# Paired rows of F on one partition in the second expert layer's weights

## The chip, the cores and the metric

The kernel runs on one core of one Trainium2 chip. The metric is device microseconds of one execution; lower is better. The kernel before takes 1385.26 us, the median of six runs between 1384.77 and 1387.1 us.

A core has a matrix engine (TensorE, PE in the profile), which multiplies a stationary operand, put in by a LDWEIGHTS instruction (its own row, PEld), with a moving operand that streams past; a vector engine (DVE); a scalar engine (ACT); GpSimd (POOL); and SyncE (SP), which here issues most of the DMAs.

## The reference

A two-dimensional Fourier mixing of 8 sequences of 2496 tokens of 256 features is followed by a mixture of experts, in which each of the 19968 tokens goes to the one of 8 experts whose logit is largest. All numbers are float32.

```python
# x: (8, 2496, 256); w_gate: (256, 8); w1: (8, 256, 1024); w2: (8, 1024, 256)
X = np.fft.fft(np.fft.fft(x, axis=1), axis=2).real.astype(np.float32).reshape(19968, 256)
logits = X @ w_gate
expert_idx = np.argmax(logits, axis=1)
probs = softmax(logits)
...
for e in range(E):                       # tokens of one expert
    h = np.maximum(x_sorted[lo:hi] @ w1[e], 0.0)
    y_sorted[lo:hi] = h @ w2[e]
return gate_w[:, None] * y               # in the order of the tokens
```

The middle dimension, F = 1024, is summed over in the second product. Any order of its 1024 rows gives the same result up to rounding, as long as the columns of `w1[e]` and the rows of `w2[e]` follow the same order.

## The kernel before, in words

The work has two parts that are woven into each other. The first part, batch by batch, computes the Fourier mixing as matmuls (`first`, `second`), finds each token's expert (`route`), and scatters the token's row, with its number and its gate weight, into a table `Xs` in HBM where each expert has its own region. The second part, `experts` (L533), takes blocks of rows of one expert from `Xs` and runs the two layers on them. There are 66 blocks: 28 of 512 rows, 13 of 256 and 25 of 128. The first six are small (two of 256, four of 128), then come four of 256, then 28 of 512, and the last stage has 7 of 256 and 21 of 128, in turn one of 256 and three of 128.

For each block, `fetch` (L507) reads the block's row number and expert from a small table into registers of SP and issues three DMAs on SP's queue: the token rows `xb` from `Xs` (L512), all of the expert's `w1` into `w1_sb` (L515, 1 MB) and all of its `w2` into `w2_sb` (L517, 1 MB). `xb`, `w1_sb` and `w2_sb` have three buffers each, so that up to two blocks ahead are loaded while one is worked on. In the profile both weight tiles are called `w_sb`.

In SBUF a tile lies over 128 partitions. `w1_sb` is [128, 2, 1024]: partition p has rows p and 128 + p of `w1` (the 256 features), each 1024 floats that lie together in HBM. `w2_sb` is [128, 8, 256]: partition p has rows p, 128 + p, ..., 896 + p of `w2`, each a separate run of 256 floats, 1 KB.

A block is computed like this:

- `turn` (L520) turns the rows with matmuls against an identity (tile `pt`, L528) and copies them as `xT` (L529), so that features lie on partitions.
- First layer: for each chunk of 128 of the 1024 columns, two products (`c` = 0, 1, the two halves of the 256 features) sum in PSUM to `ph`, with 128 columns of `w1_sb` as the stationary operand and `xT` as the moving one, as wide as the block has rows (L566). A ReLU writes the result to `hT`, on ACT for even groups (L572) and on DVE for odd ones (L570). `hT[:, f]` holds the chunk f of F on its partitions.
- Second layer: for each 128 rows of the block, eight products sum over the eight chunks to `py`, with `hT[:, f, ...]` as the stationary operand and `w2_sb[:, f]`, 256 wide, as the moving one (L584). ACT scales by the gate weight (L585) and POOL scatters the rows to `out` (L212).

All matmuls that go through the helper `mm` carry its line, L197. A float32 product is issued as two LDWEIGHTS and two MATMULs, so a block has 32 pairs for `ph` and 16 for each `py`.

The order of the instructions on each engine is the order in which the Python program issues them (a manual schedule). `experts` and the Fourier part are generators; the loop at L674 to L688 takes steps of `experts` and, by a count of work due, steps of the Fourier part of the next batch between them. Nothing of this order depends on durations or on the layout of the weights. After the seventh batch's blocks there is no Fourier work left, and the last blocks of 512 and the whole last stage are expert work alone.

Of the kernel before, what the change touches and what calls it, by code (L numbers as in the profile page):

```python
# [49 lines left out]
def bc(ap, axis, n):  # L50
    shape = list(ap.shape)
    shape.insert(axis, n)
    return ap[tuple([slice(None)] * axis + [None])].to_broadcast(shape)
# [138 lines left out]
def kernel(ctx: ExitStack, tc, x, w_gate, w1, w2, out):  # L192
    nc = tc.nc
    vec, act, pool = nc.vector, nc.scalar, nc.gpsimd

    def mm(o, lhsT, rhs, start=True, stop=True, **kw):
        nc.tensor.matmul(o, lhsT=lhsT, rhs=rhs, start=start, stop=stop, **kw)  # L197
# [13 lines left out]
    def put_row(dst, idx, rows, last, group):  # L211
        return unordered(pool.indirect_dma_start(  # L212
            out=dst, out_offset=bass.IndirectOffsetOnAxis(ap=idx, axis=0),
            in_=rows, in_offset=None, bounds_check=last, oob_is_err=False), group)
# [6 lines left out]
    def taken(ins, b):  # L221
        ins = getattr(ins, "ins", ins)
        if b + 1 < B:
            tc.declare_no_dep(ins, group=f"xs{b + 1}", reason="a block has rows of its round's batches alone")
        tc.add_to_no_dep_group("taken", ins)
# [281 lines left out]
    def fetch(b, size, tab, i):  # L507
        n = size // 128
        row = nc.sync.value_load(tab[:, 0, i:i + 1], min_val=0, max_val=ROWS - size)
        ev = nc.sync.value_load(tab[:, 1, i:i + 1], min_val=0, max_val=E - 1)  # L510
        xb = bp.tile([128, BIG // 128, W], F32, tag="xb", name="xb", bufs=3)
        taken(nc.sync.dma_start(out=xb[:, 0:n].rearrange("p t c -> p (t c)"),  # L512
                                in_=Xs[ds(row, size)].rearrange("(p t) c -> p (t c)", t=n)), b)
        w1_sb = bp.tile([128, 2, F], F32, tag="w1", name="w1_sb", bufs=3)
        nc.sync.dma_start(out=w1_sb[:], in_=w1[ds(ev, 1)].rearrange("o (c p) f -> p (o c) f", p=128))  # L515
        w2_sb = bp.tile([128, FC, D], F32, tag="w2", name="w2_sb", bufs=3)
        nc.sync.dma_start(out=w2_sb[:], in_=w2[ds(ev, 1)].rearrange("o (c p) d -> p (o c) d", p=128))  # L517
        return xb, w1_sb, w2_sb

    def turn(size, xb):  # L520

        xT = bp.tile([128, 2, BIG], F32, tag="xT", name="xT", bufs=1)
        n = min(size // 128, 2)
        for h in range(-(-size // 256)):
            pt = pst.tile([128, 2, n, 128], F32, tag="t", name="pt")
            for c in range(2):
                for t in range(n):
                    nc.tensor.transpose(pt[:, c, t], xb[:, 2 * h + t, c * 128:(c + 1) * 128], ident[:])  # L528
            vec.tensor_scalar(xT[:, :, 256 * h:256 * h + 128 * n], pt[:].rearrange("p c t k -> p c (t k)"),  # L529
                              con["alt"][:], None, op0=ALU.mult)  # L530
            yield xT

    def experts(todo):  # L533

        got, xT = [], None

        def fetch_some(k, most=3):

            while k + len(got) < len(todo) and len(got) < most and todo[k + len(got)][:3] in tabs:
                b, size, last, at = todo[k + len(got)]
                got.append(fetch(b, size, tabs[b, size, last], at))

        for k, (b, size, last, at) in enumerate(todo):
            n, m = size // 128, BIG // size
            if not k:
                while todo[0][:3] not in tabs:
                    yield 0
                fetch_some(0)  # L550
                for _ in range(9):
                    yield 0
                for xT in turn(size, got[0][0]):
                    pass
            fetch_some(k)
            xb, w1_sb, w2_sb = got.pop(0)
            turned = iter(())
            follow = todo[k + 1] if k + 1 < len(todo) else None
            ro = bp.tile([128, BIG // 128], I32, tag="ro", name="ro", bufs=4)
            vec.tensor_copy(ro[:, 0:n], xb[:, 0:n, D])  # L560
            hT = bp.tile([128, FC, BIG], F32, tag="hT", name="hT", bufs=1)
            for f in range(FC // m):
                ph = psh.tile([128, m, size], F32, tag="h", name="ph")
                for j in range(m):
                    for c in range(2):
                        mm(ph[:, j], w1_sb[:, c, (m * f + j) * 128:(m * f + j + 1) * 128], xT[:, c, 0:size],  # L566
                           c == 0, c == 1)
                o = hT[:, m * f:m * (f + 1), 0:size]
                if f % 2:
                    vec.tensor_scalar(o, ph[:], 0.0, None, op0=ALU.max)  # L570
                else:
                    act.activation(o, ph[:], ACTF.Relu)  # L572
                yield 1
            if follow:
                while follow[:3] not in tabs:
                    yield 0
                fetch_some(k + 1, 2)
                turned = turn(follow[1], got[0][0])
            y = bp.tile([128, BIG // 128, D], F32, tag="y", name="y", bufs=3)
            for i in range(n):  # L580
                xT = next(turned, xT)
                py = psy.tile([128, D], F32, tag="y", name="py")
                for f in range(FC):
                    mm(py[:], hT[:, f, i * 128:(i + 1) * 128], w2_sb[:, f], f == 0, f == FC - 1)  # L584
                act.activation(y[:, i], py[:], ACTF.Copy, scale=xb[:, i, D + 1:D + 2])  # L585
                put_row(out, ro[:, i:i + 1], y[:, i], NT - 1, "out")
                yield 2
            for xT in turned:
                pass
# [45 lines left out]
    for _ in range(WARM):  # L635
# [9 lines left out]
        out=Xs[E * CAP:].rearrange("(k p) w -> p k w", k=BLK // 128), in_=bc(pad[:], 1, BLK // 128)), "xs"), 0)  # L645
# [24 lines left out]
    for k, _ in enumerate(second(0)):  # L670
        if k % 2 == 0:
            next(early, None)
    work = experts(todo)
    for b in range(1, B):  # L674

# [40 lines left out]
```

## Time and profile before

One execution was taken with the hardware profiler.

| | |
|---|---|
| median of six runs | 1385.26 us |
| the profiled execution's own time | 1381.19 us |
| its span, first to last instruction | 1379.4 us |
| mean granted TensorE clock in it | 0.984 of full |
| HBM read, written | 194.28 MB, 54.83 MB |
| DMA packets | 134517, of them 114438 on the queue that SP issues to (q1) |
| loads of expert weights (w1 and w2) | 132 of 1024 KB |

How to read the profile: a line of the instruction groups has the line of the kernel, the engine, the operation, the tile written and the tiles read, the shapes, the count, then busy time and the mean length of one, and the idle time of the engine before these instructions with what ended it. A wait line has the total in us, how many times, and the longest. The ends of matmuls are modelled, so that one matmul's length overlaps the next one's; the time from start to start is what a matmul really takes of the engine. A weight load can run under the matmul before it. "From issue to landing" is the time from a DMA's issue to its last byte's arrival.

By stretches of the span, DMA's mean busy share is 1.04 from 100 to 150 us, 0.41 from 700 to 750 us, and 0.77 from 1130 to 1370 us.

### The profile page before, as it was taken

To read this page: it belongs to the slowest core of one execution; us is meant where nothing else is said; L and a number is where in the kernel's file an instruction comes from. 1 tells how busy PE (TensorE), PEld (TensorE's weight loads), DVE (VectorE), ACT (ScalarE), POOL (GpSimd) and SP (SyncE) were. 2 spreads that over 40 slices of the span, in tenths; PEclk is the share of its full clock that TensorE was granted. 3 is DMA by queue.
4 is the path that set the end of the run, shared out by engine and by line. 5 is a ranking of instruction groups with operands and counts; after the bars stand their busy time and mean duration, and the time that the engine had idled before them with its cause. 6 is when DMAs were issued, how large, how long until landed. Compare 5 with 4: busy or idle time off the path is not lost.

```text
span 1379.4 us, 17245 instructions
## 1 busy us (share of the span) xinstructions
PE 1320.1 (96%) x6186; PEld 1005.3 (73%) x6186; DVE 382.4 (28%) x1206; ACT 284.0 (21%) x656; POOL 352.1 (26%) x360
## 2 busy tenths in 40 slices
PE   4659999999999999999999999999999999999998
PEld 2548988776777667766777777666776689999997
DVE  3544244432333224122232212224111111111111
ACT  1413132331222113221122112221111111111111
POOL 2254334144132411431112411431311111111111
PEclk9769999999999999999999999999999999999999
DMA  8859967754366343545235142425323428888882
GB/s 233 213 195 325 371 209 223 235 167 183 125 192 186 127 164 122 177 141 174 96 129 167 60 174 92 157 95 179 123 99 105 143 85 274 279 281 280 274 269 92
DMA packets 134517, 248.81 MB, mean 180 GB/s; under 512 B 11245, under 2 KB 93839, under 8 KB 134432
## 3 DMA queue, kind: packets, MB, share of 16 engines
q1 hardware_dynamic: 114438, 194.38, 43.8%
q0 software_dynamic: 19344, 52.37, 11.0%
q10 hardware_dynamic: 650, 0.97, 0.3%
q8 instruction: 49, 0.80, 0.2%
q14 instruction: 36, 0.29, 0.1%
HBM read 194.28 MB, written 54.83 MB: 181 GB/s over the span
## 4 chain that ended last, share of the span: by engine, by line
PE 53%; issue 31%; POOL 7%; DMA 2%; DVE 1%; POOLq 0%; ACT 0%; SPq 0%; ACTq 0%; DVEq 0%
PE py L197 23%; PE ph L197 22%; POOL out_dram L212 5%; PE p L197 4%; PE s L197 2%; POOL Xs L212 2%; PE pt L528 2%; DMA Xs<-rows,pi 1%; DMA w_sb<-in_moe_w_dram 1%; DMA xb<-Xs 0%; POOLq L212 0%; PE rk L197 0%; DVE hT L570 0%; POOLq L711 0%; DVE rows L406 0%
## 5 line engine op out<-in xcount | busy, mean ns | idle before, releaser
L197 PE MATMUL ph<-xT,w_sb 128*128 128x512 f32 (+2 forms) x2112 | 585.3, 431 | 2.2 <-DMA w_sb<-in_moe_w_dram 2.2
L197 PE MATMUL py<-w_sb,hT 128*128 128x256 f32 x2608 | 580.8, 379 | 0.0
L197 PEld LDWEIGHTS py<-w_sb,hT 128*128 128x128 f32 x2608 | 487.3, 190 | 62.0
L197 PEld LDWEIGHTS ph<-xT,w_sb 128*128 128x128 f32 x2112 | 339.9, 191 | 196.6 <-issue 178.2
L212 POOL DMA_INDIRECT out_dram<-y,ro x163 | 159.2, 977 | 828.9 <-ACT y L585 808.8
L570 DVE TENSOR_SCALAR hT<-ph 128x512 f32<-128x512 f32 x163 | 112.7, 691 | 690.3 <-PE ph L197 346.6
L585 ACT ACTIVATE y<-py,xb 128x256 f32<-128x256 f32 x163 | 77.3, 474 | 603.2 <-PE py L197 598.4
L212 POOL DMA_INDIRECT Xs<-rows,pi x160 | 159.7, 998 | 119.2 <-issue 70.9
L572 ACT ACTIVATE hT<-ph 128x512 f32<-128x512 f32 x163 | 97.3, 597 | 331.7 <-PE ph L197 331.7
L529 DVE TENSOR_SCALAR xT<-pt,table 128x512 f32<-128x512 f32 (+1 forms) x94 | 63.3, 673 | 74.2 <-PE pt L528 74.2
L197 PE MATMUL s<-xh,w 104*112 104x256 f32 (+2 forms) x208 | 58.6, 405 | 18.6 <-DVE xh L284 18.5
L197 PEld LDWEIGHTS p<-table,t 120*128 120x128 f32 x352 | 53.8, 201 | 18.4 <-issue 12.0
L404 DVE COPY lg<-p 128x16 f32<-128x16 f32 x80 | 13.9, 174 | 187.2 <-ACT zs L401 187.0
L528 PE MATMUL pt<-table,xb 128*128 128x128 f32 x326 | 51.9, 275 | 11.9 <-DMA xb<-Xs 11.9
L528 PEld LDWEIGHTS pt<-table,xb 128*128 128x128 f32 x326 | 40.4, 142 | 28.5 <-DMA xb<-Xs 13.5
L197 PEld LDWEIGHTS s<-xh,w 104*112 104x112 f32 x208 | 38.1, 197 | 30.5 <-DVE xh L284 14.4
L197 PE MATMUL p<-table,zz 128*128 128x145 f32 (+1 forms) x320 | 55.8, 299 | 3.0 <-DVE rows L406 2.3
L197 PE MATMUL p<-table,t 120*128 120x120 f32 (+1 forms) x352 | 56.2, 285 | 1.8 <-DVE rows L406 1.5
L197 PEld LDWEIGHTS p<-table,zz 128*128 128x128 f32 x320 | 45.5, 194 | 6.5 <-DVE rows L406 2.4
L406 DVE SCALAR_TENSOR_TENSOR rows<-p,zs 128x129 f32<-128x129 f32 x160 | 48.3, 343 | 1.4 <-issue 0.2
L274 POOL DMA_INDIRECT xh<-in_x_dram,ix x24 | 25.0, 1041 | 72.2 <-PE s L197 51.4
L307 ACT COPY t<-s 112x512 f32<-112x512 f32 x48 | 28.0, 584 | 53.8 <-PE s L197 53.8
(84 smaller groups left out, 335.1 us busy)
## 6 DMA issues: line engine op xcount, KB each, us to landing
w_sb<-in_moe_w_dram SPq DMA_DIRECT2D x132, 1024.0 KB, 8.1
xb<-Xs SPq DMA_DIRECT2D x28, 516.0 KB, 3.7
Td<-t SPq DMA_DIRECT2D x24, 448.0 KB, 3.4
xl<-in_x_dram SPq DMA_DIRECT2D x21, 448.0 KB, 9.6
t<-Td SPq DMA_DIRECT2D x8, 720.0 KB, 7.9
t<-Td SPq DMA_DIRECT2D x8, 600.0 KB, 8.7
xb<-Xs SPq DMA_DIRECT2D x13, 258.0 KB, 4.1
xb<-Xs SPq DMA_DIRECT2D x25, 129.0 KB, 2.6
```

What stands on the lines that cost most here:

```text
L197: nc.tensor.matmul(o, lhsT=lhsT, rhs=rhs, start=start, stop=stop, **kw)
L212: return unordered(pool.indirect_dma_start(out=dst, out_offset=bass.IndirectOffsetOnAxis(ap=idx, axis=0), in_=rows, in_offset=None, bounds ...
L274: pool.indirect_dma_start(out=xh[:].rearrange("p j d -> p (j d)"), out_offset=None, in_=xrows, in_offset=bass.IndirectOffsetOnAxis(ap=ix[: ...
L307: act.copy(t1[:, 2 * half:2 * half + 2], ps[:])
L404: vec.tensor_copy(lg[:, k:k + 2], p3[:, NY:NY + 2 * E].rearrange("p (m e) -> p m e", m=2))
L406: vec.scalar_tensor_tensor(rows[:, k + m, 0:NY], p3[:, 0:NY], zs[:, 0:1], zs[:, 1:], op0=ALU.add, op1=op)
L528: nc.tensor.transpose(pt[:, c, t], xb[:, 2 * h + t, c * 128:(c + 1) * 128], ident[:])
L529: vec.tensor_scalar(xT[:, :, 256 * h:256 * h + 128 * n], pt[:].rearrange("p c t k -> p c (t k)"), con["alt"][:], None, op0=ALU.mult)
L570: vec.tensor_scalar(o, ph[:], 0.0, None, op0=ALU.max)
L572: act.activation(o, ph[:], ACTF.Relu)
L585: act.activation(y[:, i], py[:], ACTF.Copy, scale=xb[:, i, D + 1:D + 2])
```

## The change

The second layer's weights are laid out so that partition p of a pair of chunks (2c, 2c + 1) holds two neighbouring rows of `w2`: rows 256c + 2p and 256c + 2p + 1. Two neighbouring rows lie together in HBM and now also lie together on the partition, so that the load consists of pieces of 512 floats, 2 KB, instead of 256 floats, 1 KB. There are 512 pieces a load instead of 1024.

For the two layers to agree on the order of F, chunk f of the first layer takes the columns 256(f//2) + f%2 + 2p of `w1`: every second column of a stretch of 256, the even ones for even f and the odd ones for odd f. `w1` itself is loaded as before; the stationary operand of the first layer is now read from SBUF with a step of two floats, 8 bytes.

```diff
         w2_sb = bp.tile([128, FC, D], F32, tag="w2", name="w2_sb", bufs=3)
-        nc.sync.dma_start(out=w2_sb[:], in_=w2[ds(ev, 1)].rearrange("o (c p) d -> p (o c) d", p=128))
+
+        nc.sync.dma_start(out=w2_sb[:].rearrange("p (c j) d -> p c (j d)", j=2),
+                          in_=w2[ds(ev, 1)].rearrange("o (c p j) d -> p (o c) (j d)", p=128, j=2))
         return xb, w1_sb, w2_sb
+
+    def chunk(w1_sb, c, f):
+        return w1_sb[:, c, f // 2 * 256 + f % 2:(f // 2 + 1) * 256:2]
...
-                        mm(ph[:, j], w1_sb[:, c, (m * f + j) * 128:(m * f + j + 1) * 128], xT[:, c, 0:size],
-                           c == 0, c == 1)
+                        mm(ph[:, j], chunk(w1_sb, c, m * f + j), xT[:, c, 0:size], c == 0, c == 1)
```

## The prediction

> **What bounds the kernel now.** I read five views: the busy times, TensorE's waits, the instruction groups kept apart by shape, the timeline of the last stage, and the landings of the weight loads.
>
> The busy times and the DMA queues, from the page:
>
> ```profile
> span 1379.4 us, 17245 instructions
> ...
> PE 1320.1 (96%) x6186; PEld 1005.3 (73%) x6186; DVE 382.4 (28%) x1206; ACT 284.0 (21%) x656; POOL 352.1 (26%) x360
> ...
> q1 hardware_dynamic: 114438, 194.38, 43.8%
> ```
>
> TensorE is busy for 96% of the span. That is no proof by itself, since ends of matmuls are modelled, so the next view asks what it ever waits for. TensorE's waits of 2.2 us or more in total, with what ended them (us in total, times, longest us):
>
> ```profile
> PE s L197 <- DVE xh L284: 18.5, 2, 13.4
> PE pt L528 <- DMA xb<-Xs: 11.9, 3, 10.2
> PE pr L197 <- DMA t<-Td: 9.7, 2, 6.9
> PE rk L197 <- DVE oh L427: 4.8, 3, 2.6
> PE p L197 <- DVE rows L406: 3.8, 2, 2.3
> PE ph L197 <- DMA w_sb<-in_moe_w_dram: 2.2, 1, 2.2
> ```
>
> The reader is to see that the weights are waited for once, 2.2 us; that wait ends at 99.02 us, before the first block's first matmul. The longest of the `xb` waits, 10.2 us, ends at 95.68 us and is for token rows, whose load stands ahead of the first weights on SP. After 420 us TensorE has no wait that the view lists. So this is a TensorE-bound kernel from about 100 us on, and what counts is how long each matmul keeps its slot.
>
> The instruction groups of the two products, kept apart by shape (columns: busy us, mean ns of one | idle before):
>
> ```profile
> L197 PE MATMUL py<-w_sb,hT 128*128 128x256 f32 x2608 | 580.8, 379 | 0.0
> L197 PE MATMUL ph<-xT,w_sb 128*128 128x512 f32 x896 | 396.7, 593 | 0.0
> L197 PEld LDWEIGHTS ph<-xT,w_sb 128*128 128x128 f32 x2112 | 339.9, 191 | 196.6 <-issue 178.2 <-DVE p_ni L474 1.0 <-DVE mx L420 1.0
> L197 PE MATMUL ph<-xT,w_sb 128*128 128x256 f32 x416 | 95.2, 384 | 2.2 <-DMA w_sb<-in_moe_w_dram 2.2
> L197 PE MATMUL ph<-xT,w_sb 128*128 128x128 f32 x800 | 93.4, 275 | 0.0
> ```
>
> W1 (`w_sb` in `ph`) is the operand of LDWEIGHTS; W2 (`w_sb` in `py`) is the moving one. There are 2112 loads of W1 chunks: 896 stand under 512-wide matmuls, 416 under 256-wide and 800 under 128-wide ones (28, 13 and 25 blocks of 32). The means of 275 to 593 ns overlap, so I take the slot from start to start instead. The timeline of TensorE in the last stage and around two small matmuls (start us, length us):
>
> ```profile
> 123.87 0.60 PE L197 MATMUL p<-table,t 120*128 120x120 f32 x4
> ...
> 124.31 0.67 PE L197 MATMUL p<-table,zz 128*128 128x145 f32 x4
> ...
> 253.60 0.28 PE L197 MATMUL pr<-t,table 120*120 120x6 f32 x2
> 253.74 0.88 PE L197 MATMUL p<-table,t 120*128 120x120 f32 x4
> ...
> 1291.14 3.62 PE L197 MATMUL py<-w_sb,hT 128*128 128x256 f32 x16
> 1294.59 3.73 PE L197 MATMUL ph<-xT,w_sb 128*128 128x128 f32 x32
> 1298.16 0.60 PE L528 MATMUL pt<-table,xb 128*128 128x128 f32 x4
> ```
>
> Slots: 256-wide (1294.59 - 1291.14)/16 = 216 ns; 128-wide (1298.16 - 1294.59)/32 = 112 ns. A 512-wide `ph` group of 32 runs from 611.26 to the next group at 625.00, 429 ns each. So width sets the slot for 512 and 256. For 128 it is the weight load: the 120-wide `p` matmuls, whose width alone would ask for 216 x 120/256 = 101 ns, also take (124.31 - 123.87)/4 = 110 ns, and they too load 128 columns. One contiguous float32 load of 128 columns therefore costs about 112 ns, and hides under the matmul before it with 429 - 112 = 317 ns to spare at 512, 216 - 112 = 104 ns at 256, and nothing at 128.
>
> **The change, part by part.**
>
> *W2 in 2 KB pieces.* Each load has 4 pieces of 2 KB a partition in place of 8 of 1 KB: 66 loads x 512 = 33,792 fewer pieces. What a piece's size is worth is read between 1130 and 1350 us, where DMA is busiest for long (0.77 of its time from 1130 to 1370):
>
> ```profile
> L515 SPq DMA_DIRECT2D w_sb<-in_moe_w_dram x24: 372/373/1017, 1137.4 to 1339.3; - x24
> ...
> DMA to landing us min/median/max: 5.4/6.0/6.7
> ```
>
> ```profile
> L517 SPq DMA_DIRECT2D w_sb<-in_moe_w_dram x24: 372/373/1402, 1138.0 to 1339.9; - x24
> ...
> DMA to landing us min/median/max: 7.8/8.9/10.0
> ```
>
> The three loads of a block leave SP 0.6 us apart (1136.85, 1137.44, 1138.04), and the rows' load lands 2.8 us after its issue by the same view. Counted from the first issue, the rows land at 2.8, W1 (1 MB in 4 KB pieces) at 0.6 + 6.0 = 6.6 and W2 (1 MB in 1 KB pieces) at 1.2 + 8.9 = 10.1 us. So 4 KB pieces take 3.8 us and 1 KB pieces 3.5 us a MB: size buys nothing that can be seen, and I take 0 for 2 KB. If it did buy something, the most that TensorE could get back is what it still waits for DMA once weights are moving: 2.2 us for W1 and 11.9 - 10.2 = 1.7 us for `xb`, 3.9 us. Of these W1's own wait stays, I think, because its pieces and their number are unchanged and W2 is queued behind it. What hides all the other loads is the lead: with three buffers, a block's weights are issued 13.8 us or more before its first matmul in the last stage (the rows' issue at 1136.85, the first `ph` of that block at 1150.64), against 6.6 us to W1's landing. SP's issue of a load is 0.37 us, 66 of them; nothing waits for SP there. Counts of loads, semaphores and their order stay.
>
> *Which rows go where.* Chunk f of W1 now holds columns 256(f//2) + f%2 + 2p, and partition p of W2's chunk f holds the same rows of F. The sum over F is only taken in another order; ReLU is by element. `hT`, the evictions (0.60 us ACT, 0.69 us DVE) and the second product have the same shapes and addresses. The moving reads of W2 stay contiguous 1 KB. Cost 0, with nothing that could hide one.
>
> *Chunks with a step of two.* The same 2112 LDWEIGHTS now read 128 floats 8 bytes apart. No row of before has a stepped weight load, so its price is x ns against 112, and the sum is 800 x (x - 112) + 416 x (x - 216, if positive) + 896 x (x - 429, if positive).
> - Lower end: x = 112. The same 128 columns are loaded, and a shorter load could not be used much anyway: a 128-wide matmul needs 128/256 x 216 = 108 ns. I allow no gain.
> - Upper end: the load walks the whole stretch of 256 floats that it spans, two contiguous rows' worth, x = 224: 800 x 112 = 89.6 us, plus 416 x 8 = 3.3 us, 92.9 us in all.
> - Against walking speaks the nearest row with a step on TensorE's reads, the two `pr` matmuls: their moving operand is 6 floats 1 KB apart. From the first's start to the next group's there are 0.14 us, with two 120-column loads about. Walking a stretch of 6 x 256 floats at the 216 ns a 256-wide one takes would be 1.3 us each. A step as such does not cost the stretch. I take x = 112, cost 0, and keep 224 for the range.
>
> [...]
>
> **Sum.** 0 + 0 + 0. The profiled execution took 1381.19 us (span 1379.4, 1.8 around it), 4.1 us below the median of six, 1385.26. Against its own time the sum gives 1381.2, against the median 1385.3.
>
> **The rivals.**
> 1. *Stepped loads cost more* (the other side). One mechanism, in the 25 blocks of 128 rows, where 112 ns of load fill a 112 ns slot. It decides from 2.8/800 us = 3.5 ns a load, 3% of 112. A partial price, say 1.5 times (168 ns): 800 x 56 = 44.8 us, 1430.1 us. At the full stretch: 1478.2 us. For it: no cover at all at 128 wide, and no stepped load anywhere in this trace. Against it: the `pr` row.
> 2. *DMA relief reaches TensorE.* Loads and scatters fight from 100 to 150 us, where the view by stretches has a DMA share of 1.04. All DMA-ended waits gone: 1385.3 - 3.9 = 1381.4 us. Against: those waits stand behind token rows and the first W1.
> 3. *W2 gets slower*, by the new order of pieces. In the last stage DMA is 0.77 busy; 0.23 of a block's 7.25 us is 1.67 us, so W2's 3.5 us must grow by 48% before TensorE starves. At 60% the excess is 0.4 us x 24 blocks: 1395 us. Against: pieces grow and the partition count stays 128.
>
> **How the numbers follow.** A measurement of this kernel tells about 0.2% (2.8 us) from no change. Forecast, no visible change: 0.52. Rival 1: 0.32, of which half is a partial price and half about the full stretch. Rival 2: 0.14. Rival 3: 0.02. So faster 0.14, same 0.52, slower 0.34. The forecast's own range is 1382.5 to 1388.0. The full range takes in both ends of the unknown costs, 1381.4 and 1478.2; cut at 1430, the middle of the partial prices, it would leave out 0.16 and half of the other 0.16, 0.24 in all.
>
> **What the changed profile would show.** Right: 128-wide `ph` slots at 112 ns and a 128-row block at 7.25 us; the queue q1 down by some 33,800 packets; landings as before. Rival 1: that slot above 115 ns, with LDWEIGHTS of `ph` longer, and 256- and 512-wide slots unchanged. Rival 2: shorter `ph` and `pt` waits on DMA between 95 and 420 us. Rival 3: `py` waiting for `w_sb`. The forecast is wrong above all if a float32 weight load with a step runs below the contiguous rate.

## The result, and the profile after

The changed kernel takes 1388.29 us (median of 19 runs, 1385.48 to 1392.61) against 1384.82 us of the kernel before (43 runs, 1381.52 to 1388.64). The ratio over all runs is 1.0029 (of the medians alone 1.0025), with a 95% interval of 1.0021 to 1.0037: the change makes the kernel slower, by 2.9 to 5.1 us. The profiled execution took 1389.16 us, its span is 1387.4 us, 8.0 us longer than that of the one before.

The page after: busy times, and the DMA queue that loads the weights (packets, MB, share of 16 engines).

```profile
span 1387.4 us, 17245 instructions
...
PE 1324.9 (95%) x6186; PEld 1017.9 (73%) x6186; DVE 382.4 (28%) x1206; ACT 283.7 (20%) x656; POOL 351.6 (25%) x360
...
q1 hardware_dynamic: 80646, 194.38, 42.0%
```

DVE, ACT and POOL are as busy as before to within 0.5 us. TensorE's own rows grew, PE by 4.8 us and PEld by 12.6 us. The queue has 33,792 packets fewer, exactly the pieces that were saved, and its time went from 0.438 x 1379.4 = 604 us an engine to 0.420 x 1387.4 = 583 us.

The groups of the two products after, kept apart by shape:

```profile
L197 PE MATMUL py<-w_sb,hT 128*128 128x256 f32 x2608 | 580.8, 379 | 0.0
L197 PE MATMUL ph<-xT,w_sb 128*128 128x512 f32 x896 | 396.8, 593 | 0.0
L197 PEld LDWEIGHTS ph<-xT,w_sb 128*128 128x128 f32 x2112 | 352.5, 197 | 189.8 <-issue 174.2 <-DVE p_ni L474 0.9 <-DVE mx L420 0.9
L197 PE MATMUL ph<-xT,w_sb 128*128 128x128 f32 x800 | 98.1, 281 | 0.0
L197 PE MATMUL ph<-xT,w_sb 128*128 128x256 f32 x416 | 95.3, 384 | 2.7 <-DMA w_sb<-in_moe_w_dram 2.7
```

Beside the same lines of before, which the prediction shows: the loads of W1 went from a mean of 191 to 197 ns, all 2112 of them; the 128-wide matmuls from 93.4 to 98.1 us busy, 4.7 us more; the 256- and 512-wide ones stand where they were, within 0.1 us. The second product, which reads W2, did not move.

The timeline of TensorE in the last stage after:

```profile
1286.38 3.92 PE L197 MATMUL ph<-xT,w_sb 128*128 128x128 f32 x32
1290.14 0.38 PE L533 MATMUL pt<-table,xb 128*128 128x128 f32 x2
1290.37 3.62 PE L197 MATMUL py<-w_sb,hT 128*128 128x256 f32 x16
1293.82 3.92 PE L197 MATMUL ph<-xT,w_sb 128*128 128x128 f32 x32
```

A group of 32 narrow `ph` matmuls takes 1290.14 - 1286.38 = 3.76 us, 117.5 ns each, where before it took 3.57 us, 112 ns. By the starts in the two traces, the second of a group follows the first at 109 ns in both kernels; the other 31 slots take 117.8 against 111.7 ns, 6.1 ns more. All 25 groups agree to within 2 ns, also those between 100 and 150 us, where DMA is busiest (its mean share there is 1.02). The second product's 16 take 1293.82 - 1290.37 = 3.45 us, as before, so a lower clock is not the cause. So 25 groups lost 0.19 us each, 4.7 us, which lies in the interval of the measured loss. Most of the rest of the 8.0 us of span lies ahead of anything that was changed: the first load of weights is issued at 94.3 us, against 91.6 before, and the code up to there is the same in both. Steps of four and eight, below, begin at 92.6 and 91.9 us, so the late start does not go with the step; the wait in which it shows stands in the `pr` row below.

The weight loads' landings in the last stage, W2's after (compare 7.8/8.9/10.0 before):

```profile
L518 SPq DMA_DIRECT2D w_sb<-in_moe_w_dram x24: 372/373/938, 1142.1 to 1347.4; - x24
DMA to landing us min/median/max: 7.7/8.6/9.1
```

W2 lands 0.3 us sooner, and DMA is busy for 0.73 of the stage from 1138 to 1378 us against 0.77 of the like stage before. TensorE's waits after (us in total, times, longest us) show that those which a DMA ended do not shrink:

```profile
PE pr L197 <- DMA t<-Td: 12.9, 2, 9.7
PE pt L533 <- DMA xb<-Xs: 12.0, 3, 9.7
...
PE ph L197 <- DMA w_sb<-in_moe_w_dram: 2.7, 1, 2.7
```

The one wait for weights went from 2.2 to 2.7 us, those for `xb` from 11.9 to 12.0. The `pr` waits end after at 45.8 and 72.5 us, ahead of the first weight load, and are 3.2 us longer than the 9.7 us of before: about what this execution began late.

### The profile page after: what moved, and what is told of

Same layout as the page of the kernel before. It is cut to its first block, busy times and chain, and to the rows that moved or that the text cites. A ratio compares the mean times of both kernels' runs of the same rounds, so it can differ in the third digit from the quotient of the medians.

```text
span 1387.4 us, 17245 instructions
## 1 busy us (share of the span) xinstructions
PE 1324.9 (95%) x6186; PEld 1017.9 (73%) x6186; DVE 382.4 (28%) x1206; ACT 283.7 (20%) x656; POOL 351.6 (25%) x360
## 4 chain that ended last, share of the span: by engine, by line
PE 55%; issue 30%; POOL 6%; DMA 1%; DVE 0%; POOLq 0%; ACT 0%; SPq 0%; ACTq 0%; DVEq 0%
PE py L197 23%; PE ph L197 23%; POOL out_dram L212 4%; PE p L197 4%; PE s L197 2%; POOL Xs L212 2%; PE pt L533 2%; DMA xb<-Xs 1%; DMA w_sb<-in_moe_w_dram 1%; DMA Xs<-rows,pi 0%; POOLq L212 0%; PE rk L197 0%; POOLq L715 0%; DVE rows L406 0%; PE pr L197 0%
## 5 line engine op out<-in xcount | busy, mean ns | idle before, releaser
L197 PEld LDWEIGHTS ph<-xT,w_sb 128*128 128x128 f32 x2112 | 352.5, 197 | 189.8 <-issue 174.2
```

## The experiments

The theory from the two traces, A: the whole loss is the stepped weight load where nothing covers it, in the 128-wide slots. The rival, B: the loads of W2 in their new pieces cost something too, or stepped loads cost under cover. Beside these stands the question of what a step costs and why. Each edit is shown against the changed kernel; each time is compared with the kernel before, run on the same chip.

### Only the pieces

```diff
     def chunk(w1_sb, c, f):
-        return w1_sb[:, c, f // 2 * 256 + f % 2:(f // 2 + 1) * 256:2]
+        return w1_sb[:, c, f * 128:(f + 1) * 128]
```

> W2 in 2 KB pieces as in the change, W1's chunks contiguous as before. The rows of the two layers no longer match, so the sum over F pairs wrong rows: the work is the same, the numbers are not the reference's. Theory A (the whole loss is the stepped weight load, 800 x 6 ns): 128-wide slots back at 112 ns, LDWEIGHTS of ph at 190 ns, time within 0.1% of before. Theory B (the loss, or part of it, comes with the loads of W2, for example in the first 115 us): 2 to 4 us above before with slots at 112 ns.

Measured: 1386.14 us against 1383.62 us of before on the same chip, ratio 1.0010 [0.9999, 1.0021]. The groups:

```profile
L197 PEld LDWEIGHTS ph<-xT,w_sb 128*128 128x128 f32 x2112 | 339.9, 191 | 196.7 <-issue 178.3 <-DVE mx L420 1.0 <-DVE p_ni L474 1.0
...
L197 PE MATMUL ph<-xT,w_sb 128*128 128x128 f32 x800 | 93.4, 275 | 0.0
```

The load's mean and the narrow matmuls' busy time are those of before. With 2 KB pieces alone nothing is gained; the interval still allows a loss of up to 0.2%, so this run by itself does not clear W2 (theory B).

### Only the step

```diff
-        nc.sync.dma_start(out=w2_sb[:].rearrange("p (c j) d -> p c (j d)", j=2),
-                          in_=w2[ds(ev, 1)].rearrange("o (c p j) d -> p (o c) (j d)", p=128, j=2))
+        nc.sync.dma_start(out=w2_sb[:], in_=w2[ds(ev, 1)].rearrange("o (c p) d -> p (o c) d", p=128))
```

> W1's chunks with a step of two as in the change, W2 in 1 KB pieces as before (again rows that do not match; same work). Theory A: 128-wide slots at 118 ns, 800 x 6.2 = 4.9 us above before, ratio near 1.0035. Theory B: time of before or at most half of the change's loss.

Measured: 1391.08 us, ratio 1.0047 [1.0035, 1.0060], 4.8 to 8.3 us over before. The timeline in the last stage:

```profile
1304.36 3.92 PE L197 MATMUL ph<-xT,w_sb 128*128 128x128 f32 x32
1308.11 0.60 PE L532 MATMUL pt<-table,xb 128*128 128x128 f32 x4
1308.55 3.62 PE L197 MATMUL py<-w_sb,hT 128*128 128x256 f32 x16
```

3.75 us for 32, the same 117 ns as with the change. The step without the pieces has all of the loss; the 4.7 us of the slots lies just under this interval. Set beside the change (2.9 to 5.1 us) it would give the pieces a small gain, where the run with the pieces alone left room for little but a loss: neither is shown. In this profile, too, the start is late, so the spans are best cut where the changed code begins. When the first load of weights is issued, the time from there to the end of the span, and the sum of the 128-wide slots from start to start, from the profiles (us):

| kernel | W2's pieces | first weight load | from there to the end | the 800 128-wide `ph` slots |
|---|---|---|---|---|
| before | 1 KB | 91.6 | 1287.8 | 89.3 |
| the change | 2 KB | 94.3 | 1293.1 | 94.0 |
| only the pieces | 2 KB | 92.7 | 1289.3 | 89.3 |
| only the step | 1 KB | 96.9 | 1293.6 | 94.0 |
| narrow blocks as before (below) | 1 and 2 KB | 92.8 | 1288.3 | 89.3 |

The start varies by 5.3 us though no kernel differs there. Without it, the two kernels with the step of two throughout stand 5.3 and 5.8 us above before, and the two without it in the narrow blocks 1.5 and 0.5 us; 4.7 us of the former lies in the narrow slots, and none of the latter.

### Steps of four and eight

```diff
-        nc.sync.dma_start(out=w2_sb[:].rearrange("p (c j) d -> p c (j d)", j=2),
-                          in_=w2[ds(ev, 1)].rearrange("o (c p j) d -> p (o c) (j d)", p=128, j=2))
+        nc.sync.dma_start(out=w2_sb[:].rearrange("p (c j) d -> p c (j d)", j=4),
+                          in_=w2[ds(ev, 1)].rearrange("o (c p j) d -> p (o c) (j d)", p=128, j=4))
...
-        return w1_sb[:, c, f // 2 * 256 + f % 2:(f // 2 + 1) * 256:2]
+        return w1_sb[:, c, f // 4 * 512 + f % 4:(f // 4 + 1) * 512:4]
```

> The change with four neighbouring rows: W2 in 4 KB pieces, W1's chunks with a step of four floats, 16 bytes; the result is the reference's. [...] Theory C (any step costs the same 6 ns): 118 ns, 4.9 us, 1.0035. [...]

Step of eight: the same with `j=8` and

```diff
+        return w1_sb[:, c, f // 8 * 1024 + f % 8:(f // 8 + 1) * 1024:8]
```

> The change with eight neighbouring rows: W2 in one 8 KB piece a partition, W1's chunks with a step of eight floats, 32 bytes; the result is the reference's. [...] Theory C: 118 ns, 4.9 us. [...] A theory of distance (price by the stretch spanned, 6 ns for each 128 floats passed over): 112 + 43 = 155 ns, 34 us.

Measured: 1489.64 us at four, ratio 1.0772 [1.0756, 1.0789]; 1497.47 us at eight, 1.0825 [1.0810, 1.0841]. Step four, a narrow block and a 256-row block in the timeline:

```profile
1423.34 7.52 PE L197 MATMUL ph<-xT,w_sb 128*128 128x128 f32 x32
1430.70 0.60 PE L533 MATMUL pt<-table,xb 128*128 128x128 f32 x4
1431.14 3.62 PE L197 MATMUL py<-w_sb,hT 128*128 128x256 f32 x16
1434.59 7.63 PE L197 MATMUL ph<-xT,w_sb 128*128 128x256 f32 x32
1442.06 0.38 PE L533 MATMUL pt<-table,xb 128*128 128x128 f32 x2
```

Step eight:

```profile
1406.08 7.67 PE L197 MATMUL ph<-xT,w_sb 128*128 128x128 f32 x32
1413.58 0.38 PE L533 MATMUL pt<-table,xb 128*128 128x128 f32 x2
```

At four a group of 32 takes 7.36 us, 230 ns each (233.4 without the first slot), and the 256-wide group takes 7.47 us, 233 ns each: the load is now longer than the 216 ns that the 256-wide matmul covers, and sets that slot as well. At eight it is 7.50 us, 234 ns (237.8 without the first). The sum of the prediction, with x = 233.4: 800 x (233.4 - 111.7) = 97.4 us, and 416 x (233.4 - 216) = 7.2 us, 104.6 us; measured 106.0. Added up slot by slot from the starts in the traces, step four has 94.7 us more than before in the 128-wide slots, 7.3 in the 256-wide and 5.3 in the 512-wide ones, 107.3 of the 107.5 us by which the two profiles differ from the first `ph` on. The 5.3 us lies nearly all in the first `ph` slot after a narrow matmul of the Fourier part; why it is longer there was not tried.

Theory C (any step costs the same) falls, and so does a price that goes on growing with the distance, since twice the step costs 4 ns more (237.8 against 233.4). A step of two is nearly free, 6.1 ns above the contiguous load, and a step of four is not, 121.7 ns above it.

The pieces got as large as 8 KB here. DMA time on the weights' queue fell to 0.383 x 1493.8 = 572 us an engine, and the wait for the first weights is 2.0 us. None of it is in the time: from the first `ph` on, the profile at eight is 114.4 us longer than that of before, and the busy times of the `ph` matmuls grew by 98.3 us (128-wide), 10.6 (256) and 5.6 (512), 114.5 us.

### A step of three

```diff
-        return w1_sb[:, c, f // 2 * 256 + f % 2:(f // 2 + 1) * 256:2]
+        return w1_sb[:, c, f * 80:f * 80 + 382:3]
```

> W1's chunks with a step of three floats, 12 bytes, from column 80 f on; W2 as in the change. The columns are not those of the reference's chunks (some are used twice, some never); only the work is the same. [...] Theory L2 (any step beyond two pays the full price of step four): 233 ns, 104 us. [...]

Measured, in two runs: 1433.82 us against 1384.45 of before on the same chip, ratio 1.0364 [1.0342, 1.0386]. The timeline:

```profile
1368.01 5.66 PE L197 MATMUL ph<-xT,w_sb 128*128 128x128 f32 x32
1373.50 0.38 PE L533 MATMUL pt<-table,xb 128*128 128x128 f32 x2
```

5.49 us for 32, 172 ns each (173.7 without the first), against the 176 that a price by the distance would have, on a line between 118 at two and 233 at four (an estimate from these two prices). 800 x (173.7 - 111.7) = 49.6 us, and the medians differ by 49.4; slot by slot it is 48.0 us in the narrow groups and 2.4 in the 512-wide slots. A full price from three on (233 ns, 104 us) is out. The price by the distance between two and four is not: against it speaks only the step of eight, and a price that grows up to four and then stays flat would fit all the runs.

### The narrow blocks as before

```diff
+        j = 1 if size == REST else 2
+        nc.sync.dma_start(out=w2_sb[:].rearrange("p (c j) d -> p c (j d)", j=j),
+                          in_=w2[ds(ev, 1)].rearrange("o (c p j) d -> p (o c) (j d)", p=128, j=j))
...
+    def chunk(w1_sb, c, f, size):
+        if size == REST:
+            return w1_sb[:, c, f * 128:(f + 1) * 128]
         return w1_sb[:, c, f // 2 * 256 + f % 2:(f // 2 + 1) * 256:2]
```

> The change for the blocks of 512 and 256 rows, the layout of before (1 KB pieces, contiguous chunks) for the 25 blocks of 128; the result is the reference's. Theory A (only uncovered loads cost): 128-wide slots at 112 ns, LDWEIGHTS at 196 ns in the wide blocks and 190 in the narrow ones, 256- and 512-wide slots unchanged, time within 0.1% of before. Theory B (stepped loads cost under cover too): 1312 x 6 ns = 8 us above before.

Measured: 1383.62 us against 1384.45, ratio 0.9998 [0.9989, 1.0008]. The groups:

```profile
L197 PE MATMUL ph<-xT,w_sb 128*128 128x512 f32 x896 | 396.8, 593 | 0.0
L197 PEld LDWEIGHTS ph<-xT,w_sb 128*128 128x128 f32 x2112 | 347.7, 195 | 189.8 <-issue 174.0 <-DVE p_ni L474 0.9 <-DVE mx L420 0.9
L197 PE MATMUL ph<-xT,w_sb 128*128 128x256 f32 x416 | 95.2, 384 | 2.5 <-DMA w_sb<-in_moe_w_dram 2.5
L197 PE MATMUL ph<-xT,w_sb 128*128 128x128 f32 x800 | 93.4, 275 | 0.0
```

The mean load is 195 ns, between 191 and 197, as 1312 stepped and 800 contiguous ones make it. The time is that of before. So the step is free under a 256- or 512-wide matmul, whose busy times are 95.2 and 396.8 us against 95.2 and 396.7 before, and all of the loss sits in the 25 narrow blocks: theory A is shown, and B falls for the step of two under cover. For W2's pieces, which 41 of the 66 blocks have here, the interval leaves 1.5 us of gain and 1.1 us of loss. No run points to a version that beats the kernel before: the pieces gain nothing, and the step can at best be hidden.

## Why the prediction was right or wrong

**What bounds the kernel: right.** TensorE's slots from start to start, with the widths that set them (429, 216, and 112 ns by the load), carried through every run. With the measured x, the sum 800 x (x - 112) + 416 x (x - 216) gives 49.6 us at step three and 104.6 us at step four, where 49.4 and 106.0 were measured. That it comes so close is in part luck: it counts the first slot of each group in full, which lost less, and leaves out the 512-wide slots, which cost 2.4 and 5.3 us there.

**W2 in 2 KB pieces costs and brings nothing: right, as far as the runs can tell** (alone, from 0.1 us of gain to 2.9 us of loss). 33,792 packets went, 21 us of DMA time an engine with them, and W2 lands 0.3 us sooner, in a stage where a block's weights have 13.8 us of lead. Rivals 2 and 3 did not come: no DMA wait went away, and no wait of `py` for weights is listed.

**x = 112 for a chunk with a step of two: wrong, and with it the forecast.** "I take x = 112, cost 0" is the step that failed. No run shows it for a step: the load takes 118 ns in a slot that it fills alone, 6.1 ns more than the contiguous one, so rival 1 happened, with a price far below the partial one that stood for it (168 ns). Its threshold had been worked out, 3.5 ns a load, and 6.1 is beyond it: 4.7 us, measured 2.9 to 5.1. So the forecast of no visible change, with 0.52 on it, missed, the time by 0.3 us beyond its own range up to 1388.0; the full range held the time because it reached to the uncovered load's upper end. That end, two contiguous rows' worth, 224 ns, was also no bound on steps as such, since a step of four costs 233.

**Why the argument failed.** The `pr` row spoke against walking the whole stretch, and rightly: the step of eight spans 1024 floats and costs 238 ns, not eight loads. But it could not tell 0 from 5%, since its six columns stand in a slot of 0.14 us. From a row that rules out a large price I read that there was none. At a slot with no cover, a few per cent were the whole question.

**The price over the step.** Divided by the step, 117.8, 173.7 and 233.4 ns at two, three and four come to 58.9, 57.9 and 58.4 ns for each float of the step, and 237.8 at eight to 29.7. The contiguous load at that price would be 58 ns, so something else sets its 111.7. On this reading, an estimate from these five prices, a step of two is where the growth with the step just overtakes what sets the contiguous load. What makes the price grow up to four, and by only 4 ns more at eight, was not isolated.

**The size of the loss in single profiles** was misleading: 8.0 us of span for 4.7 us of slots. The first weight load is issued between 91.6 and 96.9 us in the profiles, behind code that no kernel changed, and what moves it was not tried. Cut there, the same profiles differ by 5.3 us.

## What to carry to other kernels

The step of two was paid where the load had no cover, 6.1 ns a slot, and not under the 216 and 429 ns of the wider matmuls, so look for the narrowest use of the operand first: here 800 of 2112 weight loads, in blocks so narrow that the load fills the slot, decided alone. Larger DMA pieces showed no gain here (2 KB alone: ratio 1.0010 [0.9999, 1.0021]), where the loads have 13.8 us or more of lead in the last stage over the engine that bounds the kernel; ask what waits for them before giving anything in exchange. Where a slot is uncovered, take a zero only from a row that could have shown a few per cent.

## What the runs showed of the hardware

A float32 LDWEIGHTS of 128 columns takes, in a slot that it fills, 111.7 ns with columns side by side, 117.8 at a step of two, 173.7 at three, 233.4 at four and 237.8 at eight. The price doubles between two and four and is nearly flat after it; a step of two already costs 5%, which the prediction had at nothing. A load that outgrows its cover shows at once: at a step of four the 256-wide slots went from 216 to 233 ns. Pieces of W2 from 1 to 8 KB took the weights' queue from 604 to 572 us of time an engine, 5%.
